# First batch's mixing from V's own 32 rows, masks a slot earlier, and the upper q and k in two pieces each

## The chip, the cores and the metric

The kernel runs on one core of a Trainium2 chip. The metric is device time in microseconds. The engines are TensorE (PE), VectorE (DVE), ScalarE (ACT), GpSimd (POOL) and SyncE (SP); the last two issue most of the DMAs.

## The reference

Two blocks run one behind the other: causal attention with 16 beacon keys ahead of the tokens (8 batches, 8 heads, 576 tokens, head size 64), and a mixer with a low-rank part of rank 32 and an MLP.

```python
scores = q @ concat(beacon_k, k).T / 8        # causal over the 576 tokens, beacons always seen
x = softmax(scores) @ concat(beacon_v, v)     # heads side by side: 576 x 512 per batch
u = x + (x.T @ U @ V).T                       # U: 576 x 32, V: 32 x 576
out = u + relu(u @ w_ch1) @ w_ch2             # 512 -> 2048 -> 512
```

Everything is computed in 16 bits with sums in 32 bits; inputs and output are 32 bits.

## The kernel before

The order of the work is written out by hand: each engine executes its instructions in the order in which the program emits them, and waits on semaphores only.

Attention goes by pairs of heads. Pair p belongs to batch p // 4, chunk c = p % 4. For each pair the kernel turns q and k so that the head size lies on the partitions (`qkT_of(p)`, lines 259 and 265, copied out on VectorE, line 292), computes scores in two visits (`scores_of(p)`: `sc[0]`, `sc[1]`, line 329; exponentials on ScalarE into `expt`, line 335), masks them (`sc[2]`, lines 305 and 307 on VectorE; for pairs below 5 the mask is instead added in PSUM by PE, line 321, and `sc[2]` does nothing), and multiplies with v, one head after the other (`av_of(p)`, line 357; VectorE divides into `xb`, lines 365 and 366).

When the four pairs of a batch are done, the mixing makes `uT`, the transposed u. A head multiplies U with x into `qtp` (line 387), which VectorE copies to `qts` in 16 bits. Then `ups` (496 columns) and `uend` (the last 80 tokens) get x by matmuls with the identity (line 399) and V times `qts` on top (lines 423 and 440). In the head the four chunks of 128 channels go to four groups of 32 partitions, so V must lie four times in `Vsb`, in partitions 0, 32, 64 and 96, and `Vend` holds V's last 80 columns for each chunk in the chunk's rows, zeros elsewhere. `small_loads()` loads U and V in 32 bits; its `cast()` converts them on GpSimd (`Vsb[0:32]`, line 166) and then issues three copies of `Vsb` and four of `Vend` on SP's DMA queue (lines 170 and 171).

The MLP works on blocks of 512 tokens across batches. `mlp_units` makes 16 units that multiply `uT` by one of 16 column blocks of w1 (`gps`, line 464, four matmuls each) and then 16 that multiply by w2 (`cps`, line 489). They wait in a queue, from which `fill(n)` takes n units as filling between the attention's steps. For the first block, `part(D, upto)` starts units before the last channels of `uT` exist.

The first batch's mixing is interleaved with its last pairs. The sequence is, on PE: the first head of pair 2, the mixing's head for chunks 0 and 1, the second head of pair 2, `begin` for chunks 0 and 1 (x by the identity), the first head of pair 3, `most` and `end` for chunks 0 and 1 (V), head for chunk 2, and so on, with parts of the first MLP block between.

From pair 4 to pair 7 a loop runs one pair each: it turns pair p + 2, does the second score visit of pair p + 1, masks pair p, multiplies pair p with v and does the first score visit of pair p + 2, with a few units of the queue between.

GpSimd issues nearly all loads. Its order at the start is: beacons of k, the second pair's k, k's and q's upper half (heads 4 to 7), v's beacons, v's lower half in five pieces (by blocks of tokens), v's upper half in five, the casts of U and V, then the first quarter of w1, batch 1's k and q in halves with the second quarter of w1 between, batch 1's v with the third quarter between, the last quarter, w2, and batch 2.

Of the kernel before, what the change touches and what calls it, by code (L numbers as in the profile page):

```python
# [9 lines left out]
F16 = mybir.dt.float16  # L10
BF16 = mybir.dt.bfloat16
F32 = mybir.dt.float32
# [6 lines left out]
P = 128  # L19
# [11 lines left out]
def kernel(  # L31
# [13 lines left out]
    nc = tc.nc  # L45
    B, H, S, D = q.shape
    Nb = beacon_k.shape[2]
    DM = H * D
# [53 lines left out]
    def pst(shape, dtype, name):  # L102
        return psum.tile(shape, dtype, tag="ps", name=name)
# [87 lines left out]
    def token_load(eng, src, dst, hs):  # L191
        eng.dma_start(out=dst[0:TP, hs, :], in_=src[hs].rearrange("h (p j) d -> p h (j d)", j=TJ))
# [7 lines left out]
    def v_beacon(bsrc, vs):  # L200
        beacon_load(nc.gpsimd, bsrc, by_head(vs)[:, 0, :, 0:D], ALLH)

    def v_tokens(src, vs, hs, js=range(NT)):
        dst = by_head(vs)[:, :, hs, 0:D]
        for j in js:
            a = Nb if j == 0 else 0
            nc.gpsimd.dma_start(  # L207
                out=dst[a : a + nq[j], j, :, :], in_=src[hs, ds(q0[j], nq[j]), :].rearrange("h p d -> p h d")
            )
# [143 lines left out]
    def av_unit(b, h, ex, vs, xb):  # L353
# [13 lines left out]
            out=xb[:, :, ds(h * D, D)], in0=po[:, :, 0:D], in1=r.broadcast_to([P, NT, D]), op=ALU.mult  # L367
        )

    def mix_units(xb, u0, turned=True):  # L370


        cell = {}
        ALL = range(NCC)

        def turn():
            for j in range(NT):
                nc.sync.dma_start_transpose(  # L378
                    out=uT[:, :, ds(u0 + q0[j], nq[j])], in_=xb[: nq[j], j, :]
                )  # L380

        def head(ccs=ALL):

            qtp = pst([P, P], F32, name="qtp")
            for j in range(NT):
                for cc in ccs:
                    nc.tensor.matmul(  # L387
                        qtp[ds(R * cc, R), :], Usb[: nq[j], j, :], xb[: nq[j], j, ts(cc, P)],
                        start=(j == 0), stop=(j == NT - 1), skip_group_check=True,
                        tile_position=(0, R * cc),  # L390
                    )
            if "q" not in cell:
                cell["q"] = small.tile([P, P], F16, name="qts", tag="qts")
            rs = ds(R * ccs[0], R * len(ccs))
            nc.vector.tensor_copy(out=cell["q"][rs, :], in_=qtp[rs, :])

        def x_into(ups, cc, js, a, first):
            for j in () if turned else js:
                nc.tensor.matmul(  # L399
                    ups[:, ds(q0[j] - a, nq[j])], xb[: nq[j], j, ts(cc, P)], ident[: nq[j], : nq[j]],  # L400
                    start=first and j == js[0], stop=False, skip_group_check=True,
                )

        def settle(i, dst, ups):
            if turned:
                nc.vector.tensor_tensor(out=dst, in0=ups, in1=dst, op=ALU.add)  # L406
            elif i % 2:
                nc.vector.tensor_copy(out=dst, in_=ups)
            else:
                nc.scalar.activation(out=dst, in_=ups, func=AF.Copy)  # L410

        def begin(ccs):

            for cc in ccs:
                cell[cc] = pst([P, QM], F32, name="ups")
                x_into(cell[cc], cc, list(range(NT - 1)), 0, True)

        def most(ccs=ALL, by=range(NCC)):

            begin([cc for cc in ccs if cc not in cell])  # L420
            for cc in ccs:
                rs = ds(R * cc, R)
                nc.tensor.matmul(  # L423
                    cell[cc], cell["q"][rs, :], Vsb[rs, 0:QM], start=turned, stop=True, skip_group_check=True
                )
            for cc in ccs:
                settle(by[cc], uT[:, cc, ds(u0, QM)], cell[cc])

        def end_begin(ccs=ALL):
            cell["end", ccs[0]] = pst([P, len(ccs), nq[NT - 1]], F32, name="uend")  # L430
            for i, cc in enumerate(ccs):
                x_into(cell["end", ccs[0]][:, i, :], cc, [NT - 1], QM, i == 0)

        def end(ccs=ALL, by=1):
            if ("end", ccs[0]) not in cell:
                end_begin(ccs)
            ups = cell["end", ccs[0]]
            rs = ds(R * ccs[0], R * len(ccs))
            for i, cc in enumerate(ccs):
                nc.tensor.matmul(  # L440
                    ups[:, i, :], cell["q"][rs, :], Vend[rs, cc, :], start=turned and i == 0, stop=True,
                    skip_group_check=True,
                )
            settle(by, uT[:, ds(ccs[0], len(ccs)), ds(u0 + QM, nq[NT - 1])], ups)

        return turn, head, [most, end], (begin, end_begin)

    def mlp_units(t0, n, dst, flip, turned=True, last=False):

# [245 lines left out]
    def mix(b):  # L695

        turned = b >= NF and len(queue) >= LAG + 7
        turn, head, parts, _ = mix_units(xbs[b], S * b, turned)
        if turned:
            turn()  # L700
        n = (LAG + 3 * (b == B - 1)) if turned else 2 if b >= NF else 0
        k = 2 if turned else 1
        most, end = parts
        rest = queue[n + k + 3 :]
        queue[:] = queue[0:n] + [head] + queue[n : n + k] + [most] + queue[n + k : n + k + 3] + [end]
        for _ in range(4):
            queue.extend(rest[:1] + [None])
            del rest[:1]
        queue.extend(rest)
        feed(b)  # L710

    with tc.manual_schedule(engines={ENG.PE, ENG.Activation, ENG.DVE, ENG.SP, ENG.Pool}):
        load_first()
        cast = small_loads()
        build_masks()
        for src, dst in zip((k[0], q[0]), Ls[0][0]):
            token_load(nc.gpsimd, src, dst, HALVES[1])
        v_beacon(beacon_v[0], vss[0])
        v_tokens(v[0], vss[0], HALVES[0])
        prs[0][0] = regroup(first, 0, 0, V, act_copy, beacons=False)  # L720
        keep_warm(pst([P, 512], F32, name="idle"), IDLE[0], plain)
        t0, sc = qkT_of(0), scores_of(0)
# [39 lines left out]

        sc[1]()
        av = av_of(2)
        _, head, (most, end), (begin, end_begin) = mix_units(xbs[0], 0, False)
        act = [0] * NCC
        feed(0)
        part = state["part"]
        D0, D1, D2 = range(3)
        av[0]()  # L770
        head([0, 1])
        av[1]()
        begin([0, 1])
        end_begin([0, 1])
        av = av_of(3)
        av[0]()
        most([0, 1], act)
        end([0, 1], 0)
        head([2])
        av[1]()  # L780
        begin([2])
        end_begin([2])
        part(D0, 2)
        most([2], act)
        end([2], 0)
        head([3])
        part(D1, 2)
        begin([3])
        end_begin([3])
        most([3], act)  # L790
        end([3])
        part(D2, 2)
        for x in (D0, D1, D2):
            part(x, 3)
# [8 lines left out]
        fill(1)  # L803

        sc[1]()
        masks = sc[2]
        fill(1)
        sc = scores_of(5)
        sc[0]()
# [2 lines left out]
        for p in range(NH2, NP1):  # L812
            b, c = divmod(p, NH2)
            if c == 0:
                load_batch(b + 1)
            seq = []
            prior = masks
            if p + 2 < NP1:
                seq += [lambda i=i, p=p: qkT_of(p + 2)[i]() for i in range(2)]
            if p + 3 < NP1:  # L820
                seq.append(lambda p=p: regroup_of(p + 3))
            if p + 1 < NP1:
                seq.append(sc[1])
                masks = sc[2]
            seq += [prior] + av_of(p)
            sc = []
            if p + 2 < NP1:
                new_qT_of(p + 2)
                sc = scores_of(p + 2)
                seq.append(sc[0])  # L830
            done = 0
            for i, u in enumerate(seq):
                u()
                want = FIRST[c] * (i + 1) // len(seq)
                fill(want - done)
                done = want
            if c == NH2 - 1:
                mix(b)
# [96 lines left out]
    with tc.If(n_bad != 0, label="general"):  # L935
        with tc.For_i(0, B, 1) as bi:
            L = qk_tiles()
            qT = qkt.tile([P, NH2, S], F16, name="qT", tag="qT")
            xb = xbp.tile([P, NT, DM], F16, name="xb", tag="xb")
            emit_loads(bi, L, vss[0])  # L940
            for c in range(NH2):
                pr = [regroup(L[0], c, i, nc.vector.tensor_copy) for i in range(2)]
                for u in qkT_units(in_pair(pr), qT, kTs[0], c):
                    u()
            for h in range(H):
                safe_head(h, qT, kTs[0], vss[0], xb)
            _, head, parts, _ = mix_units(xb, 0, False)
            head()
            for u in parts:
                u()  # L950
            for t0 in range(0, S, 512):
                n = min(512, S - t0)
                for u in mlp_units(t0, n, lambda i, m, t0=t0: out[bi, ds(t0 + P * i, m), :], 0, False)[0]:
                    u()
# [30 lines left out]
```

## Time and profile before

| what | value |
|---|---|
| median of three runs | 359.12 us (358.31 to 361.14) |
| the profiled execution | 363.07 us, span 361.4 us |
| granted TensorE clock, mean | 0.99 |
| busy: PE / DVE / ACT / POOL | 351.8 / 186.6 / 167.6 / 96.3 us |
| DMA | 41.28 MB, 114 GB/s over the span |

The span runs from the first to the last instruction of the profiled execution; the time of that execution is 1.7 us longer. Busy times are sums over the whole span. In a row of a timeline the columns are start, length, engine, line, operation, output and inputs, and in brackets the idle time of the engine ahead of it and what ended it. Times of the profile are microseconds from the span's start.

### The profile page before, as it was taken

To read this page: it belongs to the slowest core of one execution; us is meant where nothing else is said; L and a number is where in the kernel's file an instruction comes from. 1 tells how busy PE (TensorE), PEld (TensorE's weight loads), DVE (VectorE), ACT (ScalarE), POOL (GpSimd) and SP (SyncE) were. 2 spreads that over 40 slices of the span, in tenths; PEclk is the share of its full clock that TensorE was granted. 3 is DMA by queue.
4 is the path that set the end of the run, shared out by engine and by line. 5 is a ranking of instruction groups with operands and counts; after the bars stand their busy time and mean duration, and the time that the engine had idled before them with its cause. 6 is when DMAs were issued, how large, how long until landed. Compare 5 with 4: busy or idle time off the path is not lost.

```text
span 361.4 us, 7830 instructions
## 1 busy us (share of the span) xinstructions
PE 351.8 (97%) x3135; PEld 175.4 (49%) x3135; DVE 186.6 (52%) x482; ACT 167.6 (46%) x361; POOL 96.3 (27%) x135
## 2 busy tenths in 40 slices
PE   8979999999999999999999999999999999999995
PEld 4654555455555444444444444444454444444443
DVE  5643675569887444464536555544745433213311
ACT  5952982267853465347535554466412302401300
POOL 8767615207257209501840310000000000000000
PEclk9996999999999999999999999999999999999999
DMA  9999999969999969998999696233013315114112
GB/s 183 86 202 172 179 204 161 189 120 93 149 70 114 195 106 113 147 181 132 133 132 201 121 115 107 87 89 67 3 70 104 68 58 89 29 58 88 32 51 72
DMA packets 144138, 41.28 MB, mean 114 GB/s; under 512 B 128992, under 2 KB 139584, under 8 KB 144096
## 3 DMA queue, kind: packets, MB, share of 16 engines
q0 software_dynamic: 87408, 18.18, 64.5%
q1 hardware_dynamic: 56464, 22.25, 32.4%
q8 instruction: 26, 0.43, 0.5%
q10 hardware_dynamic: 224, 0.30, 0.3%
q14 instruction: 16, 0.13, 0.1%
HBM read 37.37 MB, written 9.44 MB: 130 GB/s over the span
## 4 chain that ended last, share of the span: by engine, by line
PE 86%; DMA 6%; DVE 3%; POOL 2%; SPq 2%; issue 1%; POOLq 0%
PE gps L464 34%; PE cps L489 32%; PE po L357 7%; PE sps L329 7%; DMA uT<-xb 2%; DMA Vend<-Vsb 2%; DMA st<-in_q_dram 2%; SPq L378 1%; PE tps L259 1%; PE qtp L387 1%; PE cph L514 1%; PE ups L423 1%; POOL vs L207 1%; PE ups L399 1%; PE tps L265 1%
## 5 line engine op out<-in xcount | busy, mean ns | idle before, releaser
L335 ACT ACTIVATE expt<-sps 128x496 f16<-128x496 f32 (+2 forms) x256 | 111.2, 539 | 58.1 <-PE sps L329 58.0
L464 PE MATMUL gps<-uT,w 128*128 128x512 f16 x576 | 137.9, 384 | 0.0
L489 PE MATMUL cps<-w,gT 128*128 128x512 f16 x560 | 132.6, 380 | 0.0
L477 ACT ACTIVATE gT<-gps 128x512 f16<-128x512 f32 x86 | 52.0, 610 | 96.0 <-PE gps L464 94.2
L464 PEld LDWEIGHTS <-w 128*128 128x128 f16 x576 | 52.1, 98 | 60.7 <-issue 5.9
L489 PEld LDWEIGHTS <-gT 128*128 128x128 f16 x560 | 49.9, 98 | 59.2 <-issue 6.9
L479 DVE TENSOR_SCALAR gT<-gps 128x512 f16<-128x512 f32 x58 | 40.0, 690 | 49.7 <-PE gps L464 48.6
L502 DVE TENSOR_TENSOR ob<-cps,ut 128x512 f32<-128x512 f32 x31 | 21.4, 689 | 49.6 <-PE cps L489 46.7
L207 POOL DMA_DIRECT2D vs<-in_v_dram x50 | 39.5, 804 | 21.7 <-DMA st<-in_k_dram 6.2
L357 PEld LDWEIGHTS <-expt 128*128 128x128 f16 (+1 forms) x960 | 36.5, 98 | 17.3 <-issue 3.3
L357 PE MATMUL po<-vs,expt 128*128 128x65 f16 (+1 forms) x960 | 40.1, 194 | 1.8 <-DVE expt L305 1.1
L329 PE MATMUL sps<-qT,kT 64*128 64x80 f16 (+4 forms) x384 | 34.2, 282 | 0.2
L366 DVE TENSOR_TENSOR xb<-po,rec 128x320 f16<-128x320 f32 x64 | 31.5, 492 | 2.2
L305 DVE TENSOR_TENSOR expt<-expt,bigmask 128x512 f16<-128x512 f16 x54 | 22.6, 419 | 11.7 <-ACT expt L335 11.7
L365 DVE RECIPROCAL rec<-po 128x5 f32<-128x5 f32 x64 | 12.0, 187 | 24.9 <-PE po L357 23.9
L329 PEld LDWEIGHTS <-kT 64*128 64x128 f16 x384 | 11.8, 94 | 20.9 <-issue 13.0
L189 POOL DMA_DIRECT2D vs<-in_beacon_v_dram x8 | 4.3, 538 | 60.4 <-PE po L357 60.4
L572 POOL DMA_DIRECT2D st<-in_q_dram x20 | 16.9, 863 | 4.0 <-DMA vs<-in_v_dram 2.9
L572 POOL DMA_DIRECT2D st<-in_k_dram x20 | 16.9, 873 | 0.7 <-DMA vs<-in_v_dram 0.7
L406 DVE TENSOR_TENSOR uT<-ups,uT 128x496 f16<-128x496 f32 x20 | 12.1, 666 | 7.0 <-PE ups L423 3.6
L292 DVE COPY qT<-tps 128x576 f16<-128x576 f16 (+1 forms) x16 | 11.8, 735 | 5.1 <-PE tps L259 2.9
L292 DVE COPY kT<-tps 128x576 f16<-128x576 f16 (+1 forms) x16 | 11.7, 734 | 2.9 <-PE tps L265 2.1
(84 smaller groups left out, 146.5 us busy)
## 6 DMA issues: line engine op xcount, KB each, us to landing
out_dram<-ob SPq DMA_DIRECT2D x35, 256.0 KB, 2.1
vs<-in_v_dram POOLq DMA_DIRECT2D x18, 128.0 KB, 7.9
w<-in_moe_w_ch_dram POOLq DMA_DIRECT2D x4, 512.0 KB, 5.9
w<-in_moe_w_ch_dram POOLq DMA_DIRECT2D x2, 1024.0 KB, 13.0
st<-in_k_dram POOLq DMA_DIRECT2D x12, 128.0 KB, 7.6
st<-in_q_dram POOLq DMA_DIRECT2D x12, 128.0 KB, 10.1
st<-in_k_dram POOLq DMA_DIRECT2D x2, 576.0 KB, 12.6
st<-in_q_dram POOLq DMA_DIRECT2D x2, 576.0 KB, 15.0
```

What stands on the lines that cost most here:

```text
L207: nc.gpsimd.dma_start(out=dst[a : a + nq[j], j, :, :], in_=src[hs, ds(q0[j], nq[j]), :].rearrange("h p d -> p h d"))
L292: copy(out=whole[:, :, ds(w * a, w)], in_=ps[:, 0 : TP * w].rearrange("x (j p) -> x p j", j=w),)
L305: nc.vector.tensor_tensor(out=e4, in0=e4, in1=bigmask, op=ALU.min)
L329: nc.tensor.matmul(ps[g, i][:, ds(o, w)], kT[hp, c, ds(P * ch, P)], qT[hp, c, ds(qa, w)], start=not early, stop=True, skip_group_check=early,)
L335: nc.scalar.activation(out=ex[i][:, ds(SLOT * g, gw[g])], in_=ps[g, i][:, 0 : gw[g]], func=AF.Exp, scale=scale)
L357: nc.tensor.matmul(po[:, j, :], ex[0 : nk[c], ds(blk[(c, j)], P)], vs[0 : nk[c], ds(c * H * E + h * E, E)], start=(c == 0), stop=(c == j),)
L366: nc.vector.tensor_tensor(out=xb[:, :, ds(h * D, D)], in0=po[:, :, 0:D], in1=r.broadcast_to([P, NT, D]), op=ALU.mult)
L464: nc.tensor.matmul(g[:, 0:n], w1[:, cc, ts(dc, P)], uT[:, cc, ds(t0, n)], start=(cc == 0), stop=(cc == NCC - 1))
L477: nc.scalar.activation(out=gT["t"][:, dc, 0:n], in_=g[:, 0:n], func=AF.Relu)
L479: nc.vector.tensor_scalar_max(out=gT["t"][:, dc, 0:n], in0=g[:, 0:n], scalar1=0.0)
L489: nc.tensor.matmul(ps[:m, :], gT["t"][:, dc, ds(P * i, m)], w2[:, dc, :], start=(dc == 0), stop=turned and dc == NDC - 1, skip_group_check ...
L572: nc.gpsimd.dma_start(out=dst[a : m[j], j, :, :], in_=src[:, ds(q0[j], nq[j]), :].rearrange("h p d -> p h d"))
```

## The change

Four things change.

1. The first batch's mixing is a function of its own, `first_mix`. The head puts the chunks side by side in the same 32 partitions (chunks 0 and 1 in one matmul of 256 columns per token block), and the copies go to `qfirst`, a tile of the output pool. `rest` multiplies with `Vsb[0:32]`, both for the first 496 columns and the last 80. The spread copies are still made by `cast()`; later batches read them.
2. `mix_units` loses the parts that served the interleaving, and otherwise does the same as before.
3. In the loop over pairs 4 to 7, the masks of the pair whose second score visit has just been emitted stand at the end of the same iteration, not in the next one ahead of that pair's `av_of`.
4. The upper half of the first batch's k and q (heads 4 to 7) is loaded in two pieces of two heads each; v's beacons and lower half stand between the first pieces and the second.

```diff
+    def first_mix(xb):
+        qts = outp.tile([P, DM], F16, name="qfirst", tag="ob")
+        cell = {}
+        def head(c0, n):
+            qtp = pst([R, P * n], F32, name="qtp")
+            for j in range(NT):
+                nc.tensor.matmul(
+                    qtp, Usb[: nq[j], j, :], xb[: nq[j], j, ds(P * c0, P * n)], start=(j == 0), stop=(j == NT - 1)
+                )
+            nc.vector.tensor_copy(out=qts[0:R, ds(P * c0, P * n)], in_=qtp)
+        def begin(c0, n):
+            for cc in range(c0, c0 + n):
+                cell[cc] = pst([P, QM], F32, name="ups")
+                x_into(xb, cell[cc], cc, list(range(NT - 1)), 0, True)
+            cell["end"] = pst([P, n, NL], F32, name="uend")
+            for i in range(n):
+                x_into(xb, cell["end"][:, i, :], c0 + i, [NT - 1], QM, i == 0)
+        def rest(c0, n, end):
+            for at in (0, QM):
+                for i in range(n):
+                    nc.tensor.matmul(
+                        cell["end"][:, i, :] if at else cell[c0 + i], qts[0:R, ts(c0 + i, P)],
+                        Vsb[0:R, at : S if at else QM], start=False, stop=True, skip_group_check=True,
+                    )
+            for cc in range(c0, c0 + n):
+                act_copy(uT[:, cc, 0:QM], cell[cc])
+            end(out=uT[:, ds(c0, n), QM:S], in_=cell["end"])
...
-        for src, dst in zip((k[0], q[0]), Ls[0][0]):
-            token_load(nc.gpsimd, src, dst, HALVES[1])
-        v_beacon(beacon_v[0], vss[0])
-        v_tokens(v[0], vss[0], HALVES[0])
+        for c in (2, 3):
+            for src, dst in zip((k[0], q[0]), Ls[0][0]):
+                token_load(nc.gpsimd, src, dst, SETS[c])
+            if c == 2:
+                v_beacon(beacon_v[0], vss[0])
+                v_tokens(v[0], vss[0], HALVES[0])
...
-        head([0, 1])
+        head(0, 2)
         av[1]()
-        begin([0, 1])
-        end_begin([0, 1])
+        begin(0, 2)
         av = av_of(3)
         av[0]()
-        most([0, 1], act)
-        end([0, 1], 0)
-        head([2])
+        rest(0, 2, act_copy)
+        head(2, 1)
...
-            prior = masks
+            masks = lambda: None
...
-            seq += [prior] + av_of(p)
+            seq += av_of(p)
             sc = []
             if p + 2 < NP1:
                 new_qT_of(p + 2)
                 sc = scores_of(p + 2)
                 seq.append(sc[0])
+            seq.append(masks)
```

More of the change, by code (lines that the diff above doesn't have):

```diff
@@ L368, in av_unit, with x_into @@
         )
+    def x_into(xb, ups, cc, js, a, first):
+        for j in js:
+            nc.tensor.matmul(
+                ups[:, ds(q0[j] - a, nq[j])], xb[: nq[j], j, ts(cc, P)], ident[: nq[j], : nq[j]],
+                start=first and j == js[0], stop=False, skip_group_check=True,
+            )
     def mix_units(xb, u0, turned=True):
         cell = {}
-        ALL = range(NCC)
         def turn():
@@ L380, in turn, with head @@
                 )
-        def head(ccs=ALL):
+        def head():
             qtp = pst([P, P], F32, name="qtp")
             for j in range(NT):
-                for cc in ccs:
+                for cc in range(NCC):
                     nc.tensor.matmul(
@@ L391, in head @@
                     )
[L392 to L402, printed above, removed]
+            qts = small.tile([P, P], F16, name="qts", tag="qts")
+            nc.vector.tensor_copy(out=qts, in_=qtp)
+            cell["q"] = qts
         def settle(i, dst, ups):
@@ L410, in settle, with most @@
                 nc.scalar.activation(out=dst, in_=ups, func=AF.Copy)
[L412 to L421, printed above, removed]
+        def most():
+            ups = [pst([P, QM], F32, name="ups") for _ in range(NCC)]
+            for cc in range(NCC) if not turned else ():
+                x_into(xb, ups[cc], cc, list(range(NT - 1)), 0, True)
+            for cc in range(NCC):
@@ L422, in most @@
                 rs = ds(R * cc, R)
                 nc.tensor.matmul(
-                    cell[cc], cell["q"][rs, :], Vsb[rs, 0:QM], start=turned, stop=True, skip_group_check=True
+                    ups[cc], cell["q"][rs, :], Vsb[rs, 0:QM], start=turned, stop=True, skip_group_check=True
                 )
[L426 to L439, printed above, removed]
+            for cc in range(NCC):
+                settle(cc, uT[:, cc, ds(u0, QM)], ups[cc])
+        def end():
+            n = nq[NT - 1]
+            ups = pst([P, NCC, n], F32, name="uend")
+            for cc in range(NCC) if not turned else ():
+                x_into(xb, ups[:, cc, :], cc, [NT - 1], QM, cc == 0)
+            for cc in range(NCC):
@@ L440, in end @@
                 nc.tensor.matmul(
-                    ups[:, i, :], cell["q"][rs, :], Vend[rs, cc, :], start=turned and i == 0, stop=True,
+                    ups[:, cc, :], cell["q"], Vend[:, cc, :], start=turned and cc == 0, stop=True,
                     skip_group_check=True,
                 )
-            settle(by, uT[:, ds(ccs[0], len(ccs)), ds(u0 + QM, nq[NT - 1])], ups)
-        return turn, head, [most, end], (begin, end_begin)
+            settle(1, uT[:, :, ds(u0 + QM, n)], ups)
@@ new lines, in mix_units @@
+        return turn, head, [most, end]
+    def first_mix(xb):
[18 more added lines that the diff above has]
+                for i in range(n):
+                    nc.tensor.matmul(
+                        cell["end"][:, i, :] if at else cell[c0 + i], qts[0:R, ts(c0 + i, P)],
+                        Vsb[0:R, at : S if at else QM], start=False, stop=True, skip_group_check=True,
+                    )
+            for cc in range(c0, c0 + n):
+                act_copy(uT[:, cc, 0:QM], cell[cc])
+            end(out=uT[:, ds(c0, n), QM:S], in_=cell["end"])
+        return head, begin, rest
@@ L697, in mix @@
         turned = b >= NF and len(queue) >= LAG + 7
-        turn, head, parts, _ = mix_units(xbs[b], S * b, turned)
+        turn, head, parts = mix_units(xbs[b], S * b, turned)
         if turned:
@@ L764 @@
         av = av_of(2)
-        _, head, (most, end), (begin, end_begin) = mix_units(xbs[0], 0, False)
-        act = [0] * NCC
+        head, begin, rest = first_mix(xbs[0])
         feed(0)
@@ L770 @@
         av[0]()
-        head([0, 1])
+        head(0, 2)
         av[1]()
-        begin([0, 1])
-        end_begin([0, 1])
+        begin(0, 2)
         av = av_of(3)
         av[0]()
-        most([0, 1], act)
-        end([0, 1], 0)
-        head([2])
+        rest(0, 2, act_copy)
+        head(2, 1)
         av[1]()
-        begin([2])
-        end_begin([2])
+        begin(2, 1)
         part(D0, 2)
-        most([2], act)
-        end([2], 0)
-        head([3])
+        rest(2, 1, act_copy)
+        head(3, 1)
         part(D1, 2)
[L788 to L791, printed above, removed]
+        begin(3, 1)
+        rest(3, 1, V)
         part(D2, 2)
@@ L805 @@
         sc[1]()
-        masks = sc[2]
         fill(1)
@@ L946 @@
                 safe_head(h, qT, kTs[0], vss[0], xb)
-            _, head, parts, _ = mix_units(xb, 0, False)
+            _, head, parts = mix_units(xb, 0, False)
             head()
```

## The prediction

> **What bounds the kernel now.** I read the page first, for the engine that fills the span, then TensorE's own waits, then its timeline around the longest of them, and last the granted clock in stretches around that place.
>
> ```profile
> span 361.4 us, 7830 instructions
> PE 351.8 (97%) x3135; PEld 175.4 (49%) x3135; DVE 186.6 (52%) x482; ACT 167.6 (46%) x361; POOL 96.3 (27%) x135
> ```
>
> TensorE (PE) is busy for 97% of the span; no other engine passes 52%. So the end comes sooner only if PE has less work, waits less, or does the same work at a higher clock. The waits of PE in the first 60 us (engine, line, who was waited for, us, times, longest):
>
> ```profile
> PE uend L440 <- DMA Vend<-Vsb: 2.0, 1, 2.0
> ...
> PE po L357 <- DVE expt L305: 1.1, 2, 0.6
> PE po L357 <- DMA vs<-in_v_dram: 0.5, 2, 0.3
> ```
>
> The largest is one wait of the first batch's mixing: the second chunk's `Vend` rows, copied by DMA into partitions 32 and up, are late. The change aims at exactly these three rows. PE's timeline shows what the first of them brings with it:
>
> ```profile
> 22.24 0.38 PE L423 MATMUL ups<-Vsb,qts 32*128 32x496 f16 x2
> 22.55 0.21 PE L440 MATMUL uend<-Vend,qts 64*128 64x80 f16 x1
> 24.81 0.19 PE L440 MATMUL uend<-Vend,qts 64*128 64x80 f16 x1 [2.05 <-DMA Vend<-Vsb]
> ...
> 26.05 0.62 PE L464 MATMUL gps<-uT,w 128*128 128x512 f16 x2
> ...
> 29.88 3.58 PE L464 MATMUL gps<-uT,w 128*128 128x512 f16 x8
> 33.39 0.71 PE L265 MATMUL tps<-ident,st 96*64 96x96 f16 x24
> 34.03 1.90 PE L464 MATMUL gps<-uT,w 128*128 128x512 f16 x8
> ```
>
> Eight matmuls of 512 columns take 3.51 us from 29.88 to 33.39 (0.44 each), while the same eight from 34.03 are done in about 1.75 (0.22 each; the next PE row begins at 35.77). Half speed, then full speed. The stretches say when (window, length, busy time of each engine, granted clock, DMA):
>
> ```profile
> 19.73:23.15 3.42, 3.03 (x70) 2.48 (x69) 2.38 (x8) 2.58 (x8) 2.15 (x4) 1.00 1.30 211
> 23.15:26.56 3.41, 1.75 (x28) 1.12 (x27) 0.81 (x3) 0.86 (x3) 1.15 (x2) 0.99 1.31 204
> 26.56:33.39 6.83, 6.83 (x26) 2.47 (x26) 1.39 (x4) 1.61 (x4) 4.13 (x7) 0.51 1.55 169
> ```
>
> A stretch of 3.41 us in which PE was busy for only 1.75 is followed by 6.83 us at a clock of 0.51; a stretch with 3.03 of 3.42 busy is followed by no drop. So the late copy costs twice: 2.05 us of waiting, and 6.83 x (1 - 0.5) = 3.4 us of half-speed work behind it.
>
> **The change part by part.**
>
> *V's own rows.* `first_mix` multiplies from `Vsb[0:32]`, which GpSimd casts; the six spread copies are still issued, but only later batches read them. The wait of 2.05 goes, and no row shows anything else that would hold the matmul at 24.81. If nothing else makes PE idle, the half-speed stretch goes too: 3.4 more. Both ends of that term: 0 if the clock falls anyway, 3.4 if not; in this execution I take 3.4, since the only 3.41 us stretch with more than 1 us idle is gone.
>
> [...]
>
> Costs of the new form, and the rows for them:
>
> ```profile
> 20.31 0.46 PE L387 MATMUL qtp<-xb,Usb 112*32 112x128 f16 x10
> 20.70 0.63 PE L357 MATMUL po<-vs,expt 128*128 128x65 f16 x15
> ...
> 22.65 1.06 ACT L410 ACTIVATE uT<-ups 128x496 f16<-128x496 f32 x2 [0.84 <-PE ups L423]
> 25.04 0.30 ACT L410 ACTIVATE uT<-uend 128x160 f16<-128x160 f32 x1 [1.32 <-PE uend L440]
> ```
>
> The head of two chunks is now 5 matmuls of 256 columns, 5 x 0.11 = 0.54 us (half of 0.22 each), against 10 of 128 in 0.39 (20.31 to 20.70): +0.15. The two `ups` matmuls took 0.31 together (22.24 to 22.55), on different rows; from the same rows each takes its own 0.21 (496 columns at 0.22 per 512), 0.42: +0.1, with 0 and 0.2 as bounds. [...] Last, the first MLP matmul (26.05) needs three ScalarE copies, 1.06 + 0.30 = 1.36 us, which can start 0.4 after the first `ups` (22.24 to 22.65): 1.8 us. PE has 1.6 to do meanwhile (0.31, two ends of about 0.1, and the 1.24 from 24.81 to 26.05). A new wait of 0.2 us, bounds 0 and 0.5. These three: -0.45.
>
> *Upper q and k pair by pair.* The lower half of v now stands behind 144 KB of k and of q instead of twice as much, so it lands sooner and the 0.5 us of the third waits row goes. ScalarE doesn't eat it: before the exponentials that follow, it idles 0.59:
>
> ```profile
> 14.87 3.38 ACT L335 ACTIVATE expt<-sps 128x496 f16<-128x496 f32 x8 [0.59 <-PE sps L329]
> ...
> 5.67 3.60 POOL L207 DMA_DIRECT2D vs<-in_v_dram  x5
> 9.82 0.71 POOL L207 DMA_DIRECT2D vs<-in_v_dram  x1 [0.54 <-DMA st<-in_k_dram]
> 11.93 2.88 POOL L207 DMA_DIRECT2D vs<-in_v_dram  x4 [1.40 <-DMA st<-in_q_dram]
> ...
> 15.90 0.76 POOL L178 DMA_DIRECT2D w<-in_moe_w_ch_dram  x1
> ```
>
> The price is two more DMA issues on GpSimd, 2 x 0.7 = 1.4 us ahead of the casts, of w1 and of all later loads. But GpSimd waits 0.54 + 1.40 = 1.94 us here, each time for the DMA issued eight before: k's and q's upper halves, v's beacons and the five of v are eight, the next issue waits for k's half and the one after it for q's. The halved pieces land earlier, so the two issues should fill these waits: between 0.5 (1.94 - 1.4) earlier and 1.4 later, I take 0.5 earlier, and nothing on the path. Pair 3's k and q now land behind v:
>
> ```profile
> 15.47 0.45 PE L265 MATMUL tps<-ident,st 96*64 96x96 f16 x12
> ```
>
> This row turns pair 3's k; it would come at 15.0. How long the five lower pieces of v took from issue to landing (min/median/max):
>
> ```profile
> DMA to landing us min/median/max: 5.4/6.2/6.6
> ```
>
> The last of the five, issued at about 8.6 (5.67 + 4 x 0.72), landed at 14.0 with the least of these. The bytes up to it are the same as those up to q's pair 3 in the new order, so I expect k at about 13 and q at 14, and no wait.
>
> *Does late data take the gain?* PE arrives about 5.5 us earlier (0.5 + 2.05 + 3.4 - 0.45) at the weights, which follow the DMA's pace. w1 in its first, second and third quarter (first the two issues from 15.9 to 18.5, then that at 30.3):
>
> ```profile
> L178 POOL DMA_DIRECT2D w<-in_moe_w_ch_dram x2: 757/774/792, 15.9 to 18.5; - x2
> DMA to landing us min/median/max: 5.6/7.8/10.1
> ...
> L178 POOL DMA_DIRECT2D w<-in_moe_w_ch_dram x1: 747/747/747, 30.3 to 30.3; - x1
> DMA to landing us min/median/max: 6.0/6.0/6.0
> ...
> 42.87 1.03 PE L464 MATMUL gps<-uT,w 128*128 128x512 f16 x4
> ```
>
> The second quarter is there at 18.5 + 10.1 = 28.6 and is first used by the second four from 34.03, at 34.9 - 5.5 = 29.4: 0.8 to spare. The third is there at 36.3 and used at 42.87 - 5.5 = 37.4: 1.1 to spare. I take no wait; the second rival prices one.
>
> *Masks a slot sooner.* Pair 5's masks now run behind scores of pair 6 instead of directly ahead of pair 5's `po`:
>
> ```profile
> 48.36 0.63 PE L357 MATMUL po<-vs,expt 128*128 128x65 f16 x15 [0.62 <-DVE expt L305]
> ...
> 50.24 0.58 PE L329 MATMUL sps<-qT,kT 64*128 64x496 f16 x4
> ...
> 55.40 1.09 PE L357 MATMUL po<-vs,expt 128*128 128x65 f16 x30 [0.45 <-DVE expt L305]
> ...
> 44.62 0.49 DVE L366 TENSOR_TENSOR xb<-po,rec 128x320 f16<-128x320 f32 x1
> 45.88 0.69 DVE L479 TENSOR_SCALAR gT<-gps 128x512 f16<-128x512 f32 x1 [0.76 <-PE gps L464]
> ...
> 47.81 0.15 DVE L297 COPY kT<-tps 128x16 f16<-128x16 f16 x1
> 47.89 0.41 DVE L305 TENSOR_TENSOR expt<-expt,bigmask 128x512 f16<-128x512 f16 x1
> ...
> 48.66 0.19 DVE L307 TENSOR_TENSOR expt<-expt,mask 80x80 f16<-80x80 f16 x1
> ```
>
> The four take 0.96 us (47.89 to 48.85) and now start when the `xb` of 44.62 is done, at 45.1, in VectorE's idle 0.76: 0.62 goes. They push the row of 45.88 and pair 7's q and k copies back by about 0.2 to 1.0; those end at 48.0 and are needed at 50.24 - 0.62 = 49.6, so 1.6 us cover them. Pair 7's masks stay behind pair 6's last `xb` on VectorE in both orders; only one of two divisions is done earlier, worth about 0.2 of the 0.45 (bounds 0 and 0.45). Together +0.8.
>
> *Sum* on the profiled execution: 2.05 + 3.4 - 0.45 + 0.5 + 0.8 = 6.3 us: 363.07 becomes 356.8, the span 355.1.
>
> That execution stands 3.95 us above the median of the runs, 359.12, and the runs themselves spread from 358.31 to 361.14. Equal waits would not spread them so; half-speed time that differs from run to run would (two lots of 3.41 us, 1.7 each). In the median run I therefore count between none and all of the 3.4, and take half: gain 6.3 - 1.7 = 4.6, 359.12 - 4.6 = 354.5.
>
> **The rivals.**
>
> *Ordinary runs have no half-speed stretch.* For it: the profiled run is 1.1% above the median. Against: the same wait stands in every run, and a run at 361.14 exists. Then only 2.9 is gained: 356.2. [...]
>
> *The lead lands in late weights.* If the two issues delay all loads by the full 1.4, the second quarter lands at 30.0 and the third at 37.7; PE waits 0.6 and 0.3, and I let pieces further back add 0.3. Gain 4.6 - 1.2 = 3.4: 355.7. For it: spare times of only 0.8 and 1.1. Against: the 1.94 us that GpSimd idles there.
>
> *Slower: pair 3's k and q come late.* They may need as long as the k and q of batch 1, issued from 16.6 to 19.9:
>
> ```profile
> DMA to landing us min/median/max: 7.9/8.6/11.5
> ```
>
> Then k, issued at 9.3 (5.67 + 3.60), lands at 17.2, and q, issued at 10.0, at 21.5 against a need at 16.2: 5.3 us of waiting near 16, and 3.4 of half-speed work behind it. 359.12 - 4.6 + 5.3 + 3.4 = 363.2. It decides from about 1.7 us of lateness (k after 16.7), where the idle share of a 3.41 us stretch reaches a half as above; below that something is still gained. Against: those pieces stood behind 512 KB of w1, these behind 288 KB of v.
>
> **How the numbers follow.** Forecast 354.5, own range 352.8 (all of the half-speed time counts) to 355.5: chance 0.53. No half-speed in ordinary runs, 356.2: 0.28. Late weights, 355.7: 0.14. Slower, 363.2: 0.05. A difference of 1%, 3.6 us, is about what a measurement of this kernel can tell from none; that is 355.5. Faster: 0.49 of the first, 0.07 and 0.06 of the next two, 0.62. Slower by over 1%: 0.03. Same: 0.35. The range reaches from 352.0 to 357.5: the forecast with 0.8 of unknown small terms below, the first rival with its masks and copies at their poor ends (1.3) above.
>
> **What would show it.** Right: no PE wait on `Vend`, none on `vs` near 13, no stretch with a granted clock near 0.5 between 20 and 35, the first turn of batch 1 (33.39) near 28, and `po` of pair 5 without a wait. Wrong: a PE wait on `st` near 15, on `w` near 29 or 37, or a drop of the clock in spite of a full PE; and if all these are gone but the timed runs fall by 3 us or less, the half-speed time was the profiled execution's own.

## The result, and the profile after

| | before | after |
|---|---|---|
| median of eight runs | 360.43 us | 357.00 us (356.65 to 357.36) |
| profiled execution: time, span | 363.07, 361.4 us | 356.95, 355.3 us |
| granted clock, mean | 0.99 | 1.00 |

One of the eight runs before took 583.52 us and is left out of the ratio; the other seven lie between 358.31 and 361.14. The ratio after to before is 0.9913, with a 95% interval from 0.9891 to 0.9936: 0.9% faster, inside the range of 352.0 to 357.5, 2.5 us above the forecast of 354.5. It lies outside the narrower range of 352.8 to 355.5 that the prediction gave its main theory, and by the prediction's own line of 1% it is "same", which had a chance of 0.35. A second set of eleven runs gave 357.07 and 0.9908 [0.9878, 0.9938]. Here and below the ratios are taken over all the runs of both sets, so they are not quite those of the medians.

The waits of PE in the first 60 us of the profile after (engine, line, who was waited for, us, times, longest):

```profile
PE idle L239 <- DVE ones L143: 1.2, 1, 1.2
PE tps L259 <- DVE pr L252: 0.4, 1, 0.4
PE po L357 <- DVE expt L305: 0.3, 1, 0.3
PE sps L321 <- ACT expt L335: 0.2, 1, 0.2
```

The wait for `Vend` and that for `vs` are gone, and the wait for masks fell from 1.1 to 0.3. PE's timeline at the place of the old wait:

```profile
19.36 0.72 PE L445 MATMUL qtp<-xb,Usb 112*32 112x256 f16 x5
20.02 0.63 PE L357 MATMUL po<-vs,expt 128*128 128x65 f16 x15
...
21.56 0.59 PE L461 MATMUL ups<-Vsb,qfirst 32*128 32x496 f16 x2
21.99 0.23 PE L461 MATMUL uend<-Vsb,qfirst 32*128 32x80 f16 x2
22.15 0.46 PE L445 MATMUL qtp<-xb,Usb 112*32 112x128 f16 x5
...
23.28 0.59 PE L487 MATMUL gps<-uT,w 128*128 128x512 f16 x2
...
25.68 1.90 PE L487 MATMUL gps<-uT,w 128*128 128x512 f16 x8
27.51 0.71 PE L265 MATMUL tps<-ident,st 96*64 96x96 f16 x24
28.15 1.90 PE L487 MATMUL gps<-uT,w 128*128 128x512 f16 x8
```

No bracket with an idle time stands in these rows. The eight matmuls of 512 columns take 1.83 us (25.68 to 27.51), where before they took 3.51. Batch 1's first turn comes at 27.51 instead of 33.39, 5.9 us sooner. In stretches (window, length, busy time of PE, its weight loads, DVE, ACT and POOL, granted clock, DMA):

```profile
18.40:21.81 3.41, 3.41 (x72) 2.77 (x71) 2.36 (x8) 2.47 (x7) 2.66 (x5) 1.00 1.25 205
21.81:25.23 3.42, 3.42 (x45) 2.13 (x43) 1.78 (x6) 1.97 (x5) 0.79 (x2) 1.00 1.31 201
25.23:28.64 3.41, 3.41 (x41) 1.65 (x39) 1.57 (x3) 1.67 (x3) 1.88 (x3) 1.00 1.29 205
```

PE is busy all the time here, and the clock stays at 1.00.

### The profile page after: what moved, and what is told of

Same layout as the page of the kernel before. It is cut to its first block, busy times and chain, and to the rows that moved or that the text cites. A ratio compares the mean times of both kernels' runs of the same rounds, so it can differ in the third digit from the quotient of the medians.

```text
span 355.3 us, 7823 instructions
## 1 busy us (share of the span) xinstructions
PE 348.2 (98%) x3130; PEld 174.2 (49%) x3130; DVE 187.3 (53%) x482; ACT 167.4 (47%) x361; POOL 97.5 (27%) x137
## 4 chain that ended last, share of the span: by engine, by line
PE 89%; DMA 3%; DVE 2%; ACT 2%; SPq 1%; issue 0%; ACTq 0%
PE gps L487 34%; PE cps L512 32%; PE po L357 8%; PE sps L329 7%; DMA uT<-xb 2%; ACT expt L335 2%; SPq L384 1%; PE tps L259 1%; DMA stk<-in_k_dram 1%; PE cph L537 1%; PE tps L265 1%; PE ups L372 1%; PE qtp L393 1%; PE sps L321 1%; PE ups L417 1%; DVE uT L404 1%
## 5 line engine op out<-in xcount | busy, mean ns | idle before, releaser
L487 PE MATMUL gps<-uT,w 128*128 128x512 f16 x576 | 135.7, 379 | 0.1
```

What stands on the lines that cost most here:

```text
L487: nc.tensor.matmul(g[:, 0:n], w1[:, cc, ts(dc, P)], uT[:, cc, ds(t0, n)], start=(cc == 0), stop=(cc == NCC - 1))
```

## The experiments

Two theories stood against each other. The first: the gain is the waits that went, and behind them half-speed time that differs from run to run. The second: the half-speed time and the spread of the kernel before have another source, and the gain is the waits alone.

**The kernel before, run by run** (no edit).

> The kernel before, unchanged, to see span and granted clock of each single run. Theory (the half-speed stretch is real and differs from run to run): the runs fall into groups by granted clock, 0.990 (6.8 us at half speed) near 361 to 363 us, 0.995 (3.4 us) about 1.7 us below, 1.000 about 3.4 us below. Rival (the spread has another source): all runs show the same clock, whatever their time.

Measured: 360.86 in the median of 12 runs, from 358.46 to 363.83. Together with the 86 runs of the same kernel that stand beside the other experiments, by granted clock:

| granted clock | runs | median, us | range |
|---|---|---|---|
| 0.997 to 1.000 | 44 | 359.77 | 358.34 to 361.14 |
| 0.992 to 0.995 | 45 | 361.05 | 359.53 to 363.33 |
| 0.989 or 0.990 | 9 | 363.06 | 361.43 to 363.88 |

One stretch of 3.41 us at half speed lowers the mean granted clock by 0.005 (1.7 of some 360 us). I take the second row for runs with one such stretch and the third for runs with two, and call this a drop. So the groups are there, 1.3 and 3.3 us apart from the first (I had expected 1.7 and 3.4). But each spreads by 2.5 to 3.8 us, so the clock isn't all of it. The profiled execution of this experiment is one of the middle group:

```profile
24.55 0.19 PE L440 MATMUL uend<-Vend,qts 64*128 64x80 f16 x1 [1.65 <-DMA Vend<-Vsb]
```

```profile
21.63:25.04 3.41, 1.76 (x32) 1.18 (x29) 1.25 (x4) 1.65 (x5) 0.97 (x2) 1.00 1.33 209
25.04:28.45 3.41, 3.41 (x31) 2.01 (x29) 0.97 (x3) 0.53 (x3) 1.80 (x3) 0.50 1.27 202
28.45:31.87 3.42, 3.42 (x35) 1.63 (x35) 1.22 (x3) 1.27 (x4) 1.83 (x3) 1.00 1.90 168
```

The first fence is the wait in PE's timeline, the second three stretches in the form shown above. A wait of 1.65 us, PE busy for 1.76 of a 3.41 us stretch, and then one stretch at half speed, not two as in the profile that the prediction reads.

**Filling the wait.** The kernel before, with unused matmuls ahead of the first `uend`:

```diff
         most([0, 1], act)
+        keep_warm(pst([P, 512], F32, name="idle"), 9)
         end([0, 1], 0)
```

> The kernel before, with nine matmuls of 512 columns into an unused PSUM tile between the two ups matmuls and the first uend matmul, so that PE is busy for 1.9 of the 2.05 us for which it waits for Vend; nothing else is changed and the wait's end is the same. Theory (the clock falls because PE idles 2.05 us): clock 1.000 in all runs, the first turn of batch 1 comes 3.4 us sooner (near 30.0), time 359.7 against 363.1 of a run with the whole stretch; runs agree within 0.7 us. Rival (the clock falls for another reason, or the wait is only lengthened): 6.8 us at 0.5 remain and the time is not lower.

Measured: 359.82 us (359.22 to 361.90), ratio 0.9988 [0.9963, 1.0014]. All 12 runs stand at 0.997 or more, where 54 of the 98 of the kernel before don't. The profile, PE's timeline and then the two stretches behind it:

```profile
21.82 2.12 PE L239 MATMUL idle<-ident 128*128 128x512 f16 x9
23.87 0.24 PE L440 MATMUL uend<-Vend,qts 64*128 64x80 f16 x2
```

```profile
21.84:25.25 3.41, 3.41 (x39) 1.99 (x38) 0.91 (x3) 1.36 (x3) 0.75 (x1) 1.00 1.30 201
25.25:28.66 3.41, 3.41 (x26) 1.49 (x24) 1.09 (x4) 1.30 (x3) 2.08 (x3) 1.00 1.30 205
```

With PE kept busy in the wait the clock doesn't fall in any of the 12 runs (lowest 0.997): it is PE's idleness there that brings the drop. It is the 12 runs that show this, not the profile: there the copy that PE waits for was issued at 16.18 and landed 6.7 us later, at 22.9, where it landed at 24.8 in the profile before, so that the wait would have been short in any case. What the filling is worth in time is not clear of zero; its median is that of the runs of the kernel before that had no drop (359.77). My expectation of runs within 0.7 us was wrong: they spread by 2.7 without any drop.

**Filling half of the wait**, with 4 in place of 9.

> The kernel before with four unused matmuls of 512 columns in the Vend wait instead of nine: PE is busy for 0.9 us of it and still idles about 1.2. Theory (the clock falls after a grid cell of 3.41 us in which PE was busy for half or less; profiles so far: 1.69 and 1.76 busy were followed by half speed, 2.32 and 2.47 were not): no cell falls below 2.1, so all runs show 0.997 or more, and the median is that of nine matmuls, 359.8. Rival (any idle stretch of over 1 us in a cell brings the drop): some runs at 0.995 or 0.990, as often as in the kernel before.

Measured: 360.34 us, ratio 0.9992 [0.9968, 1.0016]. Eleven of 12 runs at 0.997 or more; one at 0.995, the longest of all (361.95). In the profiled run PE still waits 1.2 us for `Vend`, and no drop follows:

```profile
20.41:23.83 3.42, 2.86 (x47) 1.82 (x45) 1.83 (x6) 2.01 (x5) 1.00 (x2) 1.00 1.31 210
23.83:27.24 3.41, 2.73 (x37) 1.62 (x36) 1.10 (x4) 0.85 (x3) 2.13 (x3) 1.00 1.29 203
```

The clock did as expected in nearly all runs, and the rival (any idle stretch of over 1 us brings the drop, as often as before) falls; the median lies 0.5 above that with nine, so the price isn't settled by these two.

**The mixing alone.** `first_mix` as in the change; masks and loads stand as before. The edit against the change:

```diff
-        for c in (2, 3):
-            for src, dst in zip((k[0], q[0]), Ls[0][0]):
-                token_load(nc.gpsimd, src, dst, SETS[c])
-            if c == 2:
-                v_beacon(beacon_v[0], vss[0])
-                v_tokens(v[0], vss[0], HALVES[0])
+        for src, dst in zip((k[0], q[0]), Ls[0][0]):
+            token_load(nc.gpsimd, src, dst, HALVES[1])
+        v_beacon(beacon_v[0], vss[0])
+        v_tokens(v[0], vss[0], HALVES[0])
...
+        masks = sc[2]
...
-            masks = lambda: None
+            prior = masks
...
-            seq += av_of(p)
+            seq += [prior] + av_of(p)
...
-            seq.append(masks)
```

> Only the mixing in V's own rows, masks and loads as before. Theory: 2.05 + 3.4 - 0.45 = 5.0 us below the profiled execution of before, 358.1, clock 1.000, PE waits 0.5 for vs and 1.1 for the masks remain; about 1.1 us above the whole change. Rival (the loads, not the mixing, took the wait away): the wait is still there or a new one stands in its place, time as before.

Measured: 358.73 us (357.26 to 361.15), ratio 0.9950 [0.9917, 0.9983]; two of 12 runs at 0.992 and 0.994. By the ratios this part alone carries 0.5 of the 0.9% of the whole change. The `Vend` wait is gone, as expected, but the spread is not, and the profile shows a new wait near 11:

```profile
11.00 0.45 PE L265 MATMUL tps<-ident,st 96*64 96x96 f16 x12 [0.60 <-DMA st<-in_k_dram]
```

That is pair 2's k, in one piece with pair 3's. How long these two pieces, k from 3.8 and q from 4.5, took to land:

```profile
DMA to landing us min/median/max: 7.1/7.5/7.8
```

k landed 7.1 us after its issue, at 10.9.

**Masks and loads without the mixing.** Both parts as in the change, the mixing as in the kernel before. The main lines of the edit against the change:

```diff
-        head, begin, rest = first_mix(xbs[0])
+        _, head, (most, end), (begin, end_begin) = mix_units(xbs[0], 0, False)
...
-        rest(0, 2, act_copy)
-        head(2, 1)
+        most([0, 1], act)
+        end([0, 1], 0)
+        head([2])
...
```

> The change without its mixing: masks at the end of the iteration and loads pair by pair, the first mixing as before with Vend. Theory: the Vend wait stays (PE comes 0.5 us sooner, so about 2.5 us minus what the copies gain by being issued sooner, 0.5), the clock drops in most runs, and only 0.8 to 1.3 us are gained: near 359.4 where before shows 360.4. Rival (most of the gain comes from masks and loads): 357.5 or less.

Measured: 360.22 us (358.30 to 363.52), ratio 0.9989 [0.9955, 1.0023]; seven of 12 runs have a drop. Over all runs these parts alone are worth nothing that shows. Sorted by clock something does: the five runs without a drop have a median of 358.95, 0.8 below that of the kernel before (359.77), and the five at 0.994 or 0.995 one of 360.41, 0.6 below. The wait for `Vend` is not longer: PE comes to it 0.66 sooner than in the profile before (21.89 against 22.55), and the copy lands 0.67 sooner (24.14 against 24.81). The profile taught something else as well. PE's wait, and the stretches around it:

```profile
24.14 0.19 PE L440 MATMUL uend<-Vend,qts 64*128 64x80 f16 x1 [2.04 <-DMA Vend<-Vsb]
```

```profile
19.78:23.20 3.42, 2.32 (x53) 1.84 (x50) 2.23 (x7) 2.44 (x6) 1.33 (x3) 1.00 1.29 211
23.20:26.61 3.41, 2.46 (x35) 1.51 (x34) 0.97 (x3) 0.58 (x2) 1.83 (x3) 1.00 1.30 200
26.61:30.02 3.41, 3.41 (x37) 1.68 (x37) 1.23 (x3) 1.52 (x5) 1.37 (x3) 1.00 1.56 193
```

The wait is as long as in the profile of the prediction (2.04 and 2.05), but here the border between two stretches falls into its middle. Neither is half idle, and the clock stays. The borders are counted in steps of 3.41 us from a change of the clock that the trace records, here from one behind the last matmul, at 357.70: in the profile before, changes stand at 26.49, 33.32 and 361.00, which is 2 and 96 such steps apart. Where the steps fall in the kernel differs from run to run: in the two profiles of the kernel before, the clock falls at 26.49 and at 25.04, 1.45 us apart.

**The change without its masks, and without its loads** (the lines of the mixing-alone diff that concern `masks`, and those that concern the loads), and the whole change, unedited, beside them.

> The whole change, unchanged, beside the three that follow on one chip. Theory (all that varied before were waits and the half-speed time behind them, and both are gone): 357.0, runs within 0.8 us of each other, clock 0.997 or more in all. Rival (the first runs were alike by luck): a spread of 3 us or more, as the kernel before shows.

> The change without its masks: mixing in V's own rows and loads pair by pair. Theory (each part pays its own term): 0.8 us above the whole change, 357.8, as constant as the whole; PE waits 1.1 for the masks as before. Rival (the masks also take part in the spread): a spread of over 1.5 us.

> The change without its loads: mixing in V's own rows and masks at the iteration's end. Theory (k's and q's upper halves in one piece come at different times from run to run, as one profile with only the mixing had k at 10.96 us and a PE wait of 0.6 for it): about 1 us above the whole change in the median, 358.0, with a spread of 2 us or more and a clock near 0.995 in some runs. Rival (the split is worth only its 0.5 us wait for v): 357.5, runs within 0.8 us.

| kernel | median, us | range | lowest clock | ratio to before |
|---|---|---|---|---|
| whole change | 357.07 | 356.57 to 358.80 | 0.998 | 0.9908 [0.9878, 0.9938] |
| without masks | 358.05 | 357.36 to 358.95 | 0.998 | 0.9927 [0.9896, 0.9957] |
| without loads | 358.15 | 356.73 to 359.98 | 0.993 | 0.9936 [0.9903, 0.9969] |

By the medians, masks are worth 1.0 (0.8 expected) and the loads 1.1. With 11 and 12 runs each figure is rough: drawing the runs again and again, with repeats, from those measured gives 95% intervals of 0.6 to 1.3 and 0.2 to 1.9. The loads seem to narrow the spread too: 3.3 us without them, 2.2 with them (1.4 but for one run; I had expected 0.8), and two runs with a drop, the two slowest, against none. The rival, that the split is worth its 0.5 us wait only, has its runs within 0.8 us against it, but its time of 357.5 lies inside the interval and is not excluded. The fastest run without the loads (356.73) is as fast as the whole change. What its runs of 359 to 360 wait for is not known, as the profiled execution is one of 357.03; the one wait seen is that for pair 2's k above.

**Later weights.**

```diff
         def cast():
+            for _ in range(4):
+                nc.gpsimd.tensor_copy(out=Vsb[0:R, :], in_=vf)
```

> The whole change, with four more casts of V on GpSimd ahead of the real ones (0.61 us each), so that w1 and all later loads are issued 2.4 us later; the result is the same. It prices the rival of late weights. By my spare times: batch 1's k and q land at 27.9, w1's second quarter at 30.4 and its third near 39; PE waits about 0.4, 1.0 and 1 more: 2 to 2.5 us longer, 359.2, and no drop of the clock since no 3.41 us stretch is half idle. Rival (GpSimd's issues run ahead of the DMA's pace, which decides alone): 357.0 to 357.4 and no new wait on st or w.

Measured: 359.92 us (358.74 to 360.72; 359.2 expected), 2.85 above the whole change on the same chip; no clock below 0.998. PE's timeline at the two places where it waits for w1, and at one further back:

```profile
24.07 0.60 PE L489 MATMUL gps<-uT,w 128*128 128x512 f16 x2 [0.50 <-DMA w<-in_moe_w_ch_dram]
...
30.82 1.04 PE L489 MATMUL gps<-uT,w 128*128 128x512 f16 x4 [0.83 <-DMA w<-in_moe_w_ch_dram]
...
63.29 0.43 PE L261 MATMUL tps<-ident,pr 96*128 96x96 f16 x6 [0.32 <-DVE pr L254]
```

The second quarter of w1 is late by 0.83 (expected 1.0), the first by 0.5, which I had not seen, and the regrouping of batch 2's k and q, which waits on VectorE for beacons, by 0.32; the third quarter and batch 1's k and q, for which 1 and 0.4 were expected, bring no wait. Those three are 1.65 us; the rest of the 2.85 lies further back, and its cause is not shown. So the spare time that the prediction gave the second quarter is about right: in the profile after it lands at 28.0 (issued at 17.70, 10.3 us to landing) and is first used at about 29.0, 1.0 to spare where 0.8 was worked out. A delay of 2.4 us in all loads costs about all of itself (a 95% interval, worked out as above, is 2.0 to 3.2).

Of the two theories the first holds for the half-speed time: 54 of 98 runs of the kernel before have it, and with the wait filled none of 12 has. What brought the drop in four runs of the two kernels without that wait (0.992 to 0.994, two of 12 each in the mixing alone and in the change without its loads) is not shown. For the spread it holds in part only, as runs without a drop spread too.

## Why the prediction was right or wrong

*The waits.* All three went as said, and so did the signs that were set for them: the first turn of batch 1 comes at 27.5 (28 expected), pair 5's `po` has no wait, and no stretch near 0.5 is left. (The prediction counts six spread copies; three of `Vsb` and four of `Vend` are seven.) The landings in the profile after show why nothing new came in their place. GpSimd's issues, in its timeline, and then how long pair 3's k and q took:

```profile
9.15 0.68 POOL L192 DMA_DIRECT2D st<-in_k_dram  x1
9.78 0.68 POOL L192 DMA_DIRECT2D st<-in_q_dram  x1
10.42 3.63 POOL L207 DMA_DIRECT2D vs<-in_v_dram  x5
...
15.10 0.80 POOL L178 DMA_DIRECT2D w<-in_moe_w_ch_dram  x1
```

```profile
DMA to landing us min/median/max: 4.2/4.4/4.7
```

The two added issues fill the 1.94 us that GpSimd idled, and w1 is issued 0.8 us sooner than before (15.90; expected 0.5). Pair 3's k lands at 13.3 and q at 14.4 (9.15 + 4.2, 9.78 + 4.7), against 13 and 14 in the working. The slower rival, with k at 17.2, did not come.

*The terms.* The head of two chunks costs 0.66 us instead of 0.39, so +0.27 where I took 0.15. The two `ups` matmuls cost 0.43 instead of 0.31: +0.12 against 0.1; no run shows the 0.2 that was its upper bound. The new wait for ScalarE of 0.2 did not come, since its copies end just in time:

```profile
21.97 1.06 ACT L632 ACTIVATE uT<-ups 128x496 f16<-128x496 f32 x2 [1.10 <-PE ups L461]
22.92 0.31 ACT L632 ACTIVATE uT<-uend 128x160 f16<-128x160 f32 x1
```

They end at 23.23, and the MLP's first matmul stands at 23.28. Together 0.39 against 0.45. The sum had no term for the `uend` pair: without the wait between them the two matmuls take 0.16 to the next head instead of 0.33, so the new form costs 0.22 in all. The masks gave 0.8, as the waits rows show: of pair 7's 0.45, 0.28 is left.

*The sum.* 6.3 us were expected of the profiled execution, 356.8; its counterpart after the change took 356.95. That this comes within 0.2 is in part luck, for errors cancel. PE's rows before at the head of chunk 2 and at the first matmul of w2, and then its row after at the latter:

```profile
24.93 0.46 PE L387 MATMUL qtp<-xb,Usb 112*32 112x128 f16 x5
...
57.84 0.39 PE L489 MATMUL cps<-w,gT 128*128 128x512 f16 x1
```

```profile
51.18 1.04 PE L512 MATMUL cps<-w,gT 128*128 128x512 f16 x4
```

By the head of chunks 0 and 1 PE is 0.95 ahead (20.31 before, 19.36 after; 0.13 of it by the scores near 7, ahead of all that changed), where the sum has 0.5 for the wait for `vs`. The new form costs 0.22 instead of 0.45. The half-speed time was worth 3.1 instead of 3.4: from the head of chunk 2 to the first turn of batch 1 it is 8.46 us before (24.93 to 33.39) and 5.36 after (22.15 to 27.51), while the clock stands at half for most of the first. With the 2.05 of the wait this makes 5.9 by the first turn, and 6.7 at the first matmul of w2, 0.4 more than the sum. Then 0.5 is given back, for which the sum has no term. One new wait would account for most of it; in the waits of PE over the whole span it reads

```profile
PE sps L329 <- DVE uT L404: 0.4, 2, 0.2
```

where line 404 is a later batch's mixing on VectorE.

*The step that failed*, though the range held, is the one from that execution to the median run. I set the shown median, 359.12, as what an ordinary run takes, and took half of the 3.4 us of half-speed time off it as well. With 98 runs the median is 360.4, and the half-speed time is worth 0.9 us on average (45 runs at 1.3, 9 at 3.3). The median of the three runs shown was low by chance: 359.12 is below the median even of the runs that have no drop. Both errors went the same way: the base was 1.3 us too low, and the gain, 3.4 in the medians, was put at 4.6. The sum against the profiled execution needed no such step, since the changed kernel had no drop left; taken as it was, 356.8, it would have missed by 0.2, part of that by the luck named above. The range held only through its upper end, which was set by the first rival and not by the main theory.

*The rivals.* That ordinary runs have no half-speed stretch came nearer in its number (356.2) than the forecast, but not in its mechanism: 54 of 98 have one. The prediction's sign for it was a fall of 3 us or less with all waits gone; the medians fell by 3.4, from the 359.12 that it started from only by 2.1, so this sign could not tell. Nor does the same wait stand in every run, as was said against it: the profiles have 2.05 and 1.65. The late weights cost nothing here, as the timeline after shows, and the artificial delay shows how near they were. One thing of that rival did come: VectorE waits for batch 2's beacons, hidden from PE. VectorE's timeline, and then PE's:

```profile
59.56 0.19 DVE L254 COPY pr<-st 16x128 f16<-16x128 f16 x1 [1.83 <-DMA st<-in_beacon_k_dram]
```

```profile
61.01 0.42 PE L259 MATMUL tps<-ident,pr 96*128 96x96 f16 x6
```

The regrouping behind it ends at 61.5, and PE takes its first pair at 61.01 without a wait. Little is left here of the kernel's lead over its loads.

## What to carry to other kernels

A wait of PE of about two microseconds can cost more than itself: look at the granted clock behind every such wait, and price the half-speed time as a chance, not as a constant (here 54 of 98 runs had a drop, worth 1.3 or 3.3 us). When a change takes away what varies from run to run, a sum on one profiled execution, in which the varying term is counted in full, was here the better base than an old median of three runs: off by 0.2 instead of 2.5, though in part by luck. Loads that many things wait for are best cut where their first part is needed first: the split cost two issues that ran in GpSimd's idle time, and the median fell by about 1 us.

## What the runs showed of the hardware that was not expected

In these traces the granted clock changes on a grid of 3.41 us: in the profile before it fell at 26.49 and rose at 33.32 (6.83 us at 0.50, two steps) and fell again at 361.00 (96 steps later), and in that of the repeat it stood at 0.50 for one step (25.04 to 28.45). Around the wait, a grid cell with PE busy for 1.68 us and one with 1.76 were followed by half speed, for two cells and for one; cells with 2.32, 2.46, 2.73 and 2.86 were not. This looks like a limit near half, but the busy time alone doesn't decide. At the end of the kernel, where the last matmuls run out, cells that are half idle kept the full clock. The cell of the wait in the profile before; a cell and what follows it at the end of the profile after; the same in the profile of the change without its loads:

```profile
23.08:26.49 3.41, 1.68 (x28) 1.12 (x27) 0.74 (x3) 0.93 (x3) 1.08 (x2) 1.00 1.32 204
```

```profile
349.49:352.91 3.42, 1.69 (x16) 1.27 (x13) 0.83 (x2) 0.00 (x0) 0.00 (x0) 1.00 0.40 135
352.91:355.30 2.39, 0.00 (x0) 0.00 (x0) 0.00 (x0) 0.00 (x0) 0.00 (x0) 1.00 0.03 7
```

```profile
349.60:353.02 3.42, 1.49 (x14) 1.09 (x12) 0.63 (x2) 0.00 (x0) 0.00 (x0) 1.00 0.35 114
353.02:355.37 2.35, 0.00 (x0) 0.00 (x0) 0.00 (x0) 0.00 (x0) 0.00 (x0) 1.00 0.02 5
```

Cells with 1.69 and 1.49 busy were followed by the full clock, those with 1.68 and 1.76 by half. What differs in the rows is the work: matmuls mostly of 65 to 128 columns in the cells of the wait, of 256 columns at the end. Whether the columns, the place or something else decides was not tested. Two waits of the same length, 2.05 and 2.04 us, did and did not bring a drop; where the grid falls is the difference that their rows show.

What stays open: the runs of the kernel before spread by 2.8 us without any drop, and those of the changed kernel without its loads by 3.3. One thing that the profiles show to vary is the landing of k for pairs 2 and 3. Uncut, it came 5.1 us after its issue in the profile with the filled wait, 5.7 in that of the kernel before and 7.1 in that of the mixing alone, where PE waited 0.6 for it. Cut in two, the first piece came after 4.5 to 4.7 in all five profiles. How much of the spread this explains was not measured.
